# Fused attention and mixture of experts on one core: the stretch from the last features to the second expert written out as a given order, the first expert's weights loaded during attention, and two transposes issued by ScalarE

## The chip, the cores and the metric

The kernel runs on one core of a Trainium2 chip. The metric is the device time of one execution in microseconds; a profiled execution also shows a span (first to last instruction) and the clock that was granted to TensorE. The engines are TensorE (PE; its weight loads are PEld), VectorE (DVE), ScalarE (ACT), GpSimd (POOL) and SyncE (SP), which only starts transfers. ScalarE and GpSimd can start transfers too; each engine works through its own instructions in order, so a transfer that waits holds up what stands behind it.

## The reference

Eight batches, eight heads, sequence 576, head width 64. Attention has a decay from the running sum of `log f`; its output is the input of a mixture of eight experts, of which each row takes one.

```
scores = q @ k.T / sqrt(D) + cum[:, None] - cum[None, :]     # cum = cumsum(log(clip(f)))
scores = where(causal, -1e9, scores)                          # later keys are masked
attn   = exp(scores - rowmax); attn /= attn.sum() + 1e-9
x      = (attn @ v) as [4608 rows, 512]
e      = argmax(x @ w_gate)                                   # one expert per row
out[row] = gate(row) * eom(row, e) * (relu(x[row] @ w1[e]) @ w2[e])
```

## The kernel before

**Numbers in two halves.** Values that must be exact are kept as a high half (16 bits) and a low half (the rest), so a product with a weight takes three matmuls. A weight tile is loaded as float32 (256 KB), ScalarE casts the high half and another engine subtracts for the low half (`split_w1`, `split_w2`).

**Attention.** A unit is two heads, 32 units in all. A unit takes six steps of a hand-written list (`attention()`); the table `OFF` says at which step a piece of work starts, and `order` in which sequence the pieces of one step are emitted. All engines keep that order. For each unit the row maxima come first (`maxsteps`): products of K and Q in bf16 plus a correction by the tiles `Ek` and `Eq`, which carry the decay, plus two small products of `pick` and `negm` that push masked places of a diagonal 128x128 block to a large negative number: one over the second half of the rows and 128 columns, one over 64. The negated maxima go through a transpose and three small transfers (`max_put`) into the last row of each head's half of `Eq`. The scores (`score`) are made transposed in the same manner, with `pick` and `negt`. Then exp on ScalarE, the low half of p on GpSimd or VectorE (`expo`), the products with V (`head_av`) and the division. `Ek` and `Eq` exist five times; `blank` fills them in the prologue.

**Features and routing.** When four heads of a batch are done, `feats` casts the rows to a high and a low half, `feats_turn` transposes them by transfers of 128-row tiles into `xT`, and `feats_out` writes them to the DRAM buffer `xbuf`. Per batch, `route` multiplies `xT` with the gates (`lg`), picks the expert, ranks the rows within the expert (`rk`) and scatters (row number, weight) into the table `tbl` by one GpSimd transfer for each 128 rows. Batches 0 to 5 are routed during attention, 6 and 7 after it.

**Experts.** Each expert has room for 640 rows, five tiles. `gather_ids` reads the rows' numbers from `tbl`, `gather_rows` fetches the rows from `xbuf` into `xg`, `gather_turn` transposes them, `up` makes the eight products with W1 and their ReLU halves (`up_products` on TensorE; `up_split` on ScalarE and VectorE), `down` the products with W2, the scaling and the scatter to the output. For expert 0 the first three tiles are taken from batches 0 to 5 alone (`early_gather`), so that work is there before the last batches are routed; tiles 3 and 4 (`ET` to `CT`) follow when all are routed.

**The seam.** Between attention and the loop over experts stands a block whose order is given on all engines except GpSimd. It emits, in this sequence: the loads of the first four W2 tiles of expert 0; the last features (unit `NQ - 1`), their five transposes and their write; `route(B - 1)`, advanced by `OFF["steps"]` pieces between the eight up products of the three early tiles (one piece, the `lg` products, behind product 3; then 10 and 12); the W2 splits; the ids of the last two tiles; the loads of four W1 tiles of expert 1; `down` for the three early tiles; rows and transposes of tiles 3 and 4. What follows, from the products for tiles 3 and 4 on, is ordered by the framework's planner, as is `route(B - 2)`. The W1 tiles of expert 0 are fetched and split during the end of attention, from steps 169 and 177 on (attention ends at step 192).

The framework places semaphores: from data, from buffers that are used again, and between queues.

## Time and profile before

| | us |
|---|---|
| median of three runs | 843.28 (840.65 to 843.58) |
| the profiled execution | 842.0 |
| its span | 840.3 |
| TensorE busy in the span | 763.7 |
| GpSimd, ScalarE, VectorE busy | 479.8, 342.7, 332.2 |
| attention, first to last product with V | about 14 to 374 |
| seam | about 340 to 460 |

A line of the timeline reads: start, duration, engine, line of the kernel, operation, written tile <- read tiles, partitions and elements, count; in brackets the engine's idle time ahead of it and what ended it. Starts are microseconds from the span's start. Matmuls overlap, so two starts tell more than one duration. In a group's line the two numbers behind the bar are the busy time and the mean ns of one, then the idle time ahead. In the stage table come, behind the stage and its length, busy time and count of PE, PEld, DVE, ACT and POOL, then the granted clock, the transfers' share of the 16 engines, and GB/s.

### The profile page before, as it was taken

To read this page: it belongs to the slowest core of one execution; us is meant where nothing else is said; L and a number is where in the kernel's file an instruction comes from. 1 tells how busy PE (TensorE), PEld (TensorE's weight loads), DVE (VectorE), ACT (ScalarE), POOL (GpSimd) and SP (SyncE) were. 2 spreads that over 40 slices of the span, in tenths; PEclk is the share of its full clock that TensorE was granted. 3 is DMA by queue.
4 is the path that set the end of the run, shared out by engine and by line. 5 is a ranking of instruction groups with operands and counts; after the bars stand their busy time and mean duration, and the time that the engine had idled before them with its cause. 6 is when DMAs were issued, how large, how long until landed. Compare 5 with 4: busy or idle time off the path is not lost. (4 is left out here: it accounts for less than half of the span.)

```text
span 840.3 us, 21236 instructions
## 1 busy us (share of the span) xinstructions
PE 763.7 (91%) x8814; PEld 496.9 (59%) x8814; DVE 332.2 (40%) x760; ACT 342.7 (41%) x761; POOL 479.8 (57%) x508
## 2 busy tenths in 40 slices
PE   2799999999999999766928999999999999999996
PEld 1477776777777777543515665655656566565653
DVE  5455675757575766672501221202212031120310
ACT  4145564556555645451213432424334153331420
POOL 9278678798979897741365423725437264361301
PEclk9999999999999999997968999999999999999999
DMA  4233648585868685779679544655655556444201
GB/s 146 88 114 91 159 130 158 123 166 123 166 127 161 124 167 113 93 150 161 104 151 245 173 95 141 181 127 171 159 138 166 125 169 160 123 141 101 73 14 43
DMA packets 132920, 112.61 MB, mean 134 GB/s; under 512 B 96024, under 2 KB 105426, under 8 KB 132820
## 3 DMA queue, kind: packets, MB, share of 16 engines
q1 hardware_dynamic: 121092, 75.19, 41.4%
q0 software_dynamic: 7552, 18.92, 7.8%
q10 hardware_dynamic: 4176, 17.11, 7.7%
q8 instruction: 70, 1.15, 0.6%
q14 instruction: 30, 0.25, 0.1%
HBM read 72.79 MB, written 20.48 MB: 111 GB/s over the span
## 5 line engine op out<-in xcount | busy, mean ns | idle before, releaser
L373 POOL TENSOR_TENSOR plo<-p 128x512 f16<-128x512 f32 x186 | 193.2, 1053 | 56.6 <-ACT p L371 54.1
L902 PE MATMUL hp<-xT,w1h 128*128 128x384 f16 (+1 forms) x1024 | 199.5, 305 | 24.4 <-DMA xT<-xg 23.7
L289 DVE TENSOR_REDUCE nR<-mx 128x2 f32<-128x1024 f32 (+4 forms) x160 | 126.7, 809 | 103.6 <-PE mx L263 98.9
L371 ACT ACTIVATE p<-sc 128x512 f32<-128x512 f32 x192 | 112.5, 594 | 79.7 <-PE sc L263 75.9
L902 PEld LDWEIGHTS <-w1h 128*128 128x128 f16 x1024 | 101.5, 100 | 72.9 <-DMA xT<-xg 17.1
L912 DVE SCALAR_TENSOR_TENSOR hl<-hp,hh 128x256 f16<-128x256 f32 (+1 forms) x128 | 60.5, 491 | 185.1 <-ACT hh L911 184.8
L902 PE MATMUL hp<-xT,w1l 128*128 128x384 f16 (+1 forms) x512 | 130.7, 305 | 0.0
L263 PE MATMUL sc<-qk 64*128 64x512 f32 (+4 forms) x640 | 129.1, 472 | 1.1 <-issue 1.1
L930 PE MATMUL y<-w2h,hh 128*128 128x512 f16 x320 | 120.8, 381 | 4.1 <-ACT hh L911 4.1
L931 PE MATMUL y<-w2l,hh 128*128 128x512 bf16 x320 | 121.0, 381 | 0.0
L935 POOL DMA_INDIRECT out_dram<-ys,ids x40 | 41.6, 1039 | 138.9 <-ACT ys L934 105.7
L932 PE MATMUL y<-w2h,hl 128*128 128x512 f16 x320 | 118.8, 379 | 0.0
L263 PEld LDWEIGHTS <-pick 64*128 64x128 bf16 (+1 forms) x1152 | 62.0, 98 | 47.3 <-issue 25.9
L658 POOL TENSOR_TENSOR w1l<-w1r,w1h 128x512 bf16<-128x512 f32 x56 | 63.8, 1158 | 45.1 <-ACT w1h L657 43.9
L657 ACT CAST w1h<-w1r 128x512 f16<-128x512 f32 x64 | 39.5, 617 | 119.7 <-issue 64.2
L864 DVE TENSOR_TENSOR w2l<-w2r,w2h 128x512 bf16<-128x512 f32 x36 | 27.7, 772 | 148.5 <-ACT w2h L863 148.5
L934 ACT ACTIVATE ys<-y,ids 128x512 f32<-128x512 f32 x40 | 27.3, 686 | 123.9 <-PE y L932 91.7
L263 PE MATMUL mx<-qk 64*128 64x256 bf16 (+5 forms) x384 | 62.8, 309 | 14.7 <-DVE nR L289 8.9
L447 PE MATMUL av<-Vs,plo 128*128 128x65 f16 x640 | 68.9, 192 | 6.4 <-POOL plo L373 6.4
L445 PE MATMUL av<-Vs,p 128*128 128x65 f16 x640 | 69.7, 194 | 0.9 <-ACT xr L492 0.7
L446 PE MATMUL av<-Vs,p 128*128 128x64 bf16 x640 | 69.2, 195 | 0.0
L911 ACT ACTIVATE hh<-hp 128x256 f16<-128x256 f32 (+1 forms) x128 | 50.3, 432 | 40.9 <-PE hp L902 40.0
(148 smaller groups left out, 1395.6 us busy)
## 6 DMA issues: line engine op xcount, KB each, us to landing
qk<-in_qk_dram ACTq DMA_DIRECT2D x29, 576.0 KB
w1r<-in_w_dram SPq DMA_DIRECT2D x64, 256.0 KB
w2r<-in_w_dram SPq DMA_DIRECT2D x64, 256.0 KB
v<-in_vm_dram SPq DMA_DIRECT2D x16, 576.0 KB
xbuf<-x SPq DMA_DIRECT2D x16, 512.0 KB
qk<-in_qk_dram SPq DMA_DIRECT2D x3, 576.0 KB
xT<-x SPq DMA_TRANSPOSE x72
Eq<-mts SPq DMA_DIRECT2D x64, 0.1 KB
```

What stands on the lines that cost most here:

```text
L263: nc.tensor.matmul(dst(i), w(i), x(i), start=start, stop=stop)
L289: nc.vector.tensor_reduce(o, x, axis=AX.X, op=ALU.max, negate=True)
L371: nc.scalar.activation(out=f32, in_=src, func=AF.Exp, scale=0.125)
L373: eng.tensor_tensor(lo, f32, upper(f32), op=ALU.subtract)
L445: nc.tensor.matmul(dst, ph, vv[:, 0:W], start=kc == 0, stop=False)
L446: nc.tensor.matmul(dst[:, 0:D], ph, vv[:, W:].bitcast(BF16), start=False, stop=False)
L447: nc.tensor.matmul(dst, pl, vv[:, 0:W], start=False, stop=kc == qc)
L658: (eng or nc.vector).tensor_tensor(l, raw, h, op=ALU.subtract)
L902: nc.tensor.matmul(m[:, 0:(t1 - t0) * P], w[:, k], xT[:, t0:t1, k // 2, j, k % 2], start=k == 0 and i == 0, stop=k == ND - 1 and i == 2)
L930: nc.tensor.matmul(y, hh[:, fc, sl], wh, start=fc == 0, stop=False)
L931: nc.tensor.matmul(y, hh[:, fc, sl], wl, start=False, stop=False)
L932: nc.tensor.matmul(y, hl[:, fc, sl], wh, start=False, stop=fc == NF - 1)
```

## The change

It has five parts.

1. **Masks.** Four spare rows of each half of `Ek` and `Eq` now carry a mask for one quadrant of each diagonal block (-6e4 times 6e4). The `pick` products for 128 columns shrink to 64, in the row maxima and in the scores. For it `blank(0)` has four more selects on GpSimd, and the other copies of `Eq` are made on ScalarE from `plainq`.
2. **Weights of expert 0.** W1 and W2 tiles are loaded and split in attention, two of each around steps 48, 72, 96 and 120, each fetched ten steps ahead.
3. **Early rows.** The ids are read one step after batch 5 is routed (four before), the rows five steps after that (four before).
4. **The seam in a given order on all five engines**, from the last features to the weights of expert 1: the first two transposes of the last features stand ahead of the second half's casts; W1 tiles 0 to 3 of expert 1 are loaded before the routing, 4 to 7 later; the `lg` products stand behind product 5; ids of expert 1 come along with those of tiles 3 and 4; the low halves of W1 are made on VectorE; `down` for the early tiles is cut in two; the rows of expert 1 are fetched between the pieces. A GpSimd fill of one element stands between the last scatters.
5. **Two transposes of the last features** (tiles 1 and 3) are issued by ScalarE.

```diff
-    "feats0": 19, ... "rank": 6, "w1r": 169, "w1": 177, "w1step": 2,
-    "hold": 188, "gather": 180, "ids": 4, "landed": 4, ...
+    "feats0": 19, ... "rank": 6, "w1r": 10, "w1": 48, "w1step": 2, "w2": 4,
+    "hold": 188, "gather": 180, "ids": 5, "landed": 1, ...
-    "steps": [0, 0, 0, 1, 10, 12, 0, 0], "w2from": 1, ...
+    "steps": [0, 0, 0, 0, 0, 1, 8, 1], ...
...
     def blank(i, eng=nc.gpsimd):
-        eng.memset(Eqs[i], 1.0)
         if i == 0:
+            nc.vector.memset(Eqs[0], 1.0)
             nc.vector.memset(Eks[0], 0.0)
+            for h in range(HU):
+                sl = slice(h * D + 32, h * D + 32 + NC)
+                nc.vector.memset(Eqs[0][sl], 0.0)
+                for x, half, v in ((Eqs[0], 0, -6e4), (Eks[0], 1, 6e4)):
+                    x = x[sl, 0:SM].rearrange("p (c h k) -> p c h k", h=2, k=D)[:, :, half]
+                    nc.gpsimd.affine_select(out=x, in_=x, pattern=[[-1, NC], [0, D]], compare_op=ALU.not_equal,
+                                            fill=v, base=0, channel_multiplier=1)
...
         else:
             nc.gpsimd.tensor_copy(Eks[i], plain)
+            nc.scalar.copy(out=Eqs[i], in_=plainq)
...
         nc.gpsimd.tensor_copy(plain, Eks[0])
+        nc.scalar.copy(out=plainq, in_=Eqs[0])
...
-                    (lambda i: m[:, i, o + n - P:o + n], lambda i: pick[rows(i), 0], lambda i: negm[rows(i), 0],
+                    (lambda i: m[:, i, o + n - P:o + n - D], lambda i: pick[rows(i), 0], lambda i: negm[rows(i), 0, 0:D],
...
-            out += [(lambda i: dst(i)[:, 0:P], lambda i: pick[rows(i), 1], lambda i: negt[rows(i), 1], False, True)]
+            out += [(lambda i: dst(i)[:, D:P], lambda i: pick[rows(i), 1], lambda i: negt[rows(i), 1, D:], False, True)]
...
+            eng = nc.scalar if u == NQ - 1 and t % 2 else nc.sync
+            eng.dma_start_transpose(...)
...
+            if b == B - 1 and t:
+                nc.gpsimd.memset(apart, 0.0)
             ins = nc.gpsimd.indirect_dma_start(out=tbl, ...)
...
+    def early_split2(fc):
+        raw = W2r.pop(fc)
+        ...
+        nc.scalar.copy(out=h, in_=raw)
+        nc.vector.tensor_tensor(l, raw, h, op=ALU.subtract)
...
-    with tc.manual_schedule(engines=ENGINES - {mybir.EngineType.Pool}):
-        W2r = [fetch_w2(w2[0], fc) for fc in range(4)]
+    with tc.manual_schedule(engines=ENGINES):
         for part in range(2):
             feats(NQ - 1, part)
-        for t in range(NTB):
-            feats_turn(NQ - 1, t)
+            for t in (range(2), range(2, NTB))[part]:
+                feats_turn(NQ - 1, t)
         feats_out(NQ - 1)
+        W1r = [fetch_w1(m2, w1[1], fc, 4) for fc in range(4)]
         chain = route(B - 1)
         ...
         gather_ids(ar, tbl[EARLY:CAP], CT - ET, ET, x)
-        W1r = [fetch_w1(m2, w1[1], fc, 4) for fc in range(4)]
-        down(W2, x, h, 0, ET)
+        x1 = gather_ids(m2, tbl[NT:NT + CAP], CT)
+        W1n = [load_w1(w1[1], fc, W1r, nc.vector) for fc in range(4)]
+        down(W2, x, h, 0, 2)
         for t in range(ET, CT):
             gather_rows(x, t)
             gather_turn(x, t)
+        down(W2, x, h, 2, ET)
+        for t in range(2):
+            gather_rows(x1, t)
+        W1r += [fetch_w1(m2, w1[1], fc, 4) for fc in range(4, NF)]
+        up(W1, x, [(ET, CT)], h)
+        for t in range(2, CT):
+            gather_rows(x1, t)
+        for t in range(CT):
+            gather_turn(x1, t)
+        W1n += [load_w1(w1[1], fc, W1r, nc.vector) for fc in range(4, NF)]
+        down(W2, x, h, ET, CT)
+        W1, x = W1n, x1
+        W2 = weights(load_w2, w2[1])
```

More of the change, by code (lines that the diff above doesn't have):

```diff
@@ L55 @@
     "mturn": -7, "rows": -6, "put": -5, "rscore": 2, "rexp": 3, "av": 5, "fetch_v": (-19, -25, -21), "v": ((-2, -9, -16), (1, -7, -15)), "apart": 2, "scatter": 13,
-    "feats0": 19, "feats1": 20, "fturn": 21, "fturnstep": 2, "fout": 31, "route": 45, "rank": 6, "w1r": 169, "w1": 177, "w1step": 2,
-    "hold": 188, "gather": 180, "ids": 4, "landed": 4, "gturn": 2, "route_last": 200, "nsum": 8, "nrec": 9, "nx": 9, "nrest": 10,
+    "feats0": 19, "feats1": 20, "fturn": 21, "fturnstep": 2, "fout": 31, "route": 45, "rank": 6, "w1r": 10, "w1": 48, "w1step": 2, "w2": 4,
+    "hold": 188, "gather": 180, "ids": 5, "landed": 1, "gturn": 2, "route_last": 200, "nsum": 8, "nrec": 9, "nx": 9, "nrest": 10,
     "mv": ["xr", "v0", "v1"], "begin": -18, "wg": -4, "spread/1": -11,
-    "steps": [0, 0, 0, 1, 10, 12, 0, 0], "w2from": 1, "dve": [181, 183, 185, 187, 189, 191],
-    "w1pool": [0, 1, 2, 3, 4, 5, 6, 7],
+    "steps": [0, 0, 0, 0, 0, 1, 8, 1], "dve": [181, 183, 185, 187, 189, 191],
     "order": "reduce put feats1 v0 scores nrec max pair rows spread feats0 fetch "
@@ L113, in _attn_moe @@
     Eqs = [ab.tile([P, S], F16, name=f"Eq{i}") for i in range(NB)]
-    plain = ab.tile([P, S], F16, name="plain")
+    plain, plainq = [ab.tile([P, S], F16, name=n) for n in ("plain", "plainq")]
     Vs = [ab.tile([P, VC, 2 * D + 1], F16, name=f"Vs{i}") for i in range(3)]
@@ L171, in _attn_moe @@
     late = cp.tile([P, 1], F32, name="late")
+    apart = cp.tile([1, 1], F32, name="apart")
     identh = cp.tile([P, P], F16, name="identh")
@@ L523, in feats_turn @@
             xT, x16 = xTs[u]
-            nc.sync.dma_start_transpose(xT[:, t].rearrange("p j k n -> p (j k) n"),
-                                        x16[:, t].rearrange("p j n -> p (j n)"))
+            eng = nc.scalar if u == NQ - 1 and t % 2 else nc.sync
+            eng.dma_start_transpose(xT[:, t].rearrange("p j k n -> p (j k) n"),
+                                    x16[:, t].rearrange("p j n -> p (j n)"))
     def feats_out(u):
@@ L668, in early_split, with early_fetch2 @@
         W1.append(split_w1(ar, W1r.pop(fc), NF))
+    W2, W2r = [], {}
+    def early_fetch2(fc):
+        W2r[fc] = a.tile([P, DM], F32, name="w2r", bufs=2)
+        nc.sync.dma_start(W2r[fc], w2[0][fc])
+    def early_split2(fc):
+        raw = W2r.pop(fc)
+        h = ar.tile([P, DM], F16, name="w2h", bufs=NF)
+        l = ar.tile([P, DM], BF16, name="w2l", bufs=NF)
+        nc.scalar.copy(out=h, in_=raw)
+        nc.vector.tensor_tensor(l, raw, h, op=ALU.subtract)
+        W2.append((h, l))
     def gather_ids(pool, rows, n, t0=0, x=None):
@@ L716, in attention @@
         for fc in range(NF):
-            for f, o in ((early_fetch, "w1r"), (early_split, "w1")):
-                extra.setdefault(OFF[o] + OFF["w1step"] * fc, []).append((f, fc))
+            at = OFF["w1"] + 24 * (fc // 2) + OFF["w1step"] * (fc % 2)
+            extra.setdefault(at - OFF["w1r"], []).append((early_fetch, fc))
+            extra.setdefault(at, []).append((early_split, fc))
+            at += OFF["w2"]
+            extra.setdefault(at - OFF["w1r"], []).append((early_fetch2, fc))
+            extra.setdefault(at, []).append((early_split2, fc))
         for s in range(OFF["begin"], last + OFF["nrest"] + 1):
@@ L940, in weights, with load_w1 @@
         return [load(we, fc) for fc in range(NF)]
-    def load_w1(we, fc, raws=None):
-        return split_w1(m2, raws[fc] if raws and fc < len(raws) else fetch_w1(m2, we, fc, 4), 8, nc.gpsimd if fc in OFF["w1pool"] else None)
+    def load_w1(we, fc, raws=None, eng=nc.gpsimd):
+        return split_w1(m2, raws[fc] if raws else fetch_w1(m2, we, fc, 4), 8, eng)
     x = st["early"]
-    with tc.manual_schedule(engines=ENGINES - {mybir.EngineType.Pool}):
-        W2r = [fetch_w2(w2[0], fc) for fc in range(4)]
+    with tc.manual_schedule(engines=ENGINES):
         for part in range(2):
             feats(NQ - 1, part)
-        for t in range(NTB):
-            feats_turn(NQ - 1, t)
+            for t in (range(2), range(2, NTB))[part]:
+                feats_turn(NQ - 1, t)
         feats_out(NQ - 1)
+        W1r = [fetch_w1(m2, w1[1], fc, 4) for fc in range(4)]
         chain = route(B - 1)
@@ L956, in _attn_moe @@
         h = hidden()
-        W2 = []
         for fc in range(NF):
@@ L985, in _attn_moe @@
     halves = [(0, CT // 2), (CT // 2, CT)]
-    for e in range(E):
-        if e:
+    for e in range(1, E):
+        if e > 1:
             W2 = weights(load_w2, w2[e])
-            h = up(W1, x, halves)
-        else:
-            up(W1, x, [(ET, CT)], h)
+        h = up(W1, x, halves)
+        if e == 1:
             nsl = overflow_slots()
@@ L994, in _attn_moe @@
         if e + 1 < E:
-            W1 = [load_w1(w1[e + 1], fc, None if e else W1r) for fc in range(NF)]
+            W1 = [load_w1(w1[e + 1], fc) for fc in range(NF)]
             x = gather(m2, tbl[(e + 1) * NT:(e + 1) * NT + CAP], CT)
-        down(W2, xe, h, 0 if e else ET, CT)
+        down(W2, xe, h, 0, CT)
     with tc.For_i(0, nsl, 1) as i:
```

8 lines of the change are left out of this document (removed).

## The prediction

> **What bounds the kernel now.** I read the page's totals first, then the busy times by stage, then TensorE's waits in time order where a stage was not full. The page:
>
> ```profile
> span 840.3 us, 21236 instructions
> PE 763.7 (91%) x8814; PEld 496.9 (59%) x8814; DVE 332.2 (40%) x760; ACT 342.7 (41%) x761; POOL 479.8 (57%) x508
> ```
>
> The profiled execution took 842.0 us, 1.7 above its span and 1.3 below the median 843.28 of the three runs shown. TensorE leaves 76.6 us of the span. The stage table (busy us of each engine, then granted clock and DMA share) tells where:
>
> ```profile
> 252.00:300.00 48.00, 48.00 (x921) 36.22 (x919) 33.07 (x83) 28.97 (x69) 41.80 (x45) 1.00 0.74 155
> 340.00:360.00 20.00, 13.77 (x215) 9.54 (x212) 11.46 (x22) 9.75 (x22) 14.47 (x14) 0.91 0.92 92
> 380.00:400.00 20.00, 13.48 (x96) 7.81 (x97) 5.66 (x15) 3.81 (x9) 0.97 (x2) 0.76 0.98 165
> 420.00:440.00 20.00, 3.38 (x17) 1.41 (x16) 0.00 (x0) 3.06 (x5) 11.65 (x12) 0.63 0.72 141
> 440.00:460.00 20.00, 15.92 (x87) 9.98 (x86) 3.23 (x7) 6.60 (x13) 12.81 (x12) 0.77 1.11 237
> ```
>
> Inside attention (252 to 300) TensorE is full, GpSimd at 87%, VectorE 69%, ScalarE 60%. From 340 to 460, the seam, TensorE has holes and runs at a lower clock after each. TensorE's timeline there, with what ended each hole:
>
> ```profile
> 360.06 0.39 PE L263 MATMUL sc<-Eq,Ek 64*128 64x512 f16 x2 [1.12 <-DMA Eq<-mts]
> 381.36 0.80 PE L902 MATMUL hp<-xT,w1h 128*128 128x384 f16 x2 [7.11 <-DMA xT<-xg]
> 394.21 0.19 PE L556 MATMUL lg<-wgs,xT 128*128 128x32 f16 x1 [3.37 <-DMA xT<-x]
> 397.51 0.21 PE L556 MATMUL lg<-wgs,xT 128*128 128x32 f16 x1 [0.26 <-DMA xT<-x]
> 439.77 0.61 PE L902 MATMUL hp<-xT,w1h 128*128 128x256 f16 x2 [16.62 <-DMA xT<-xg]
> 449.14 0.61 PE L930 MATMUL y<-w2h,hh 128*128 128x512 f16 x1 [4.08 <-ACT hh L911]
> ```
>
> The holes stand for the early rows' transposes (7.1), the last features' transposes before the router (3.4, and smaller ones up to 397.5), the last two row tiles of expert 0 (16.6) and ReLUs queued behind weight casts (4.1).
>
> **The change part by part.** Times are on the clock of this profile.
>
> *Prologue.* Five fills of Eq leave GpSimd and VectorE; four small selects (4 partitions, 256 wide) are added on GpSimd, two 4-partition fills on VectorE, five copies of Eq on ScalarE.
>
> ```profile
> 2.11 0.28 POOL L181 TENSOR_SCALAR_AFFINE_SELECT pick<-pick 64x128 bf16<-64x128 bf16 x1
> 4.06 0.68 ACT L150 ACTIVATE d<-d 64x576 f32<-64x576 f32 x1 [1.96 <-DVE d L149]
> 6.83 1.93 POOL L127 TENSOR_SCALAR_AFFINE_SELECT Ek<-Ek 64x576 f16<-64x576 f16 x2
> 8.82 0.77 POOL L148 COPY plain<-Ek 128x576 f16<-128x576 f16 x1
> 9.62 3.75 SPq L162 DMA_DIRECT2D Ek<-d  x6
> 13.90 1.19 PE L263 MATMUL mx<-Ek,Eq 63*128 63x512 f16 x2 [7.50 <-DMA Ek<-d]
> ```
>
> The new copy plainq<-Eqs[0] stands in ScalarE's order ahead of the Ln at 4.06, and waits for three of the new selects, which GpSimd reaches at 6.83, or about a microsecond sooner if the scan no longer runs beside it. A select is between 0.28 (128 wide) and 0.97 (576 wide); I take 0.4. So Eqs[0] is ready near 7 to 8, the copy (0.66, the nearest rows are 0.6 to 0.8) ends near 7.5 to 8.7 and the Ln moves by 3.4 to 4.7. Behind it hang the scan, the three row copies and the six Ek<-d transfers, so TensorE's 13.90 moves as far. The shorter bound is GpSimd's own path, four selects ahead of plain: 1.7. I take **+3.4** (1.7 to 4.7).
>
> *Masks.* One matmul pair of each diagonal block shrinks from 128 to 64 columns, four blocks per unit in the row maxima and four in the scores:
>
> ```profile
> 330.12 0.20 PE L263 MATMUL mx<-qk 64*64 64x64 bf16 x2
> 330.15 0.20 PE L263 MATMUL mx<-Ek,Eq 63*64 63x64 f16 x2
> 335.40 0.22 PE L263 MATMUL mx<-qk 64*128 64x128 bf16 x2
> 335.45 0.22 PE L263 MATMUL mx<-Ek,Eq 63*128 63x128 f16 x2
> ```
>
> Read the starts, not the durations, which overlap: a pair of 64 columns holds TensorE 0.03 us, one of 128 columns 0.05 to 0.055. That is 0.025 x 8 x 32 units = 6.4 at most; the first units and the last two are not TensorE-bound. **-5** (-6.4 to 0: GpSimd at 87% could become the limit).
>
> *Weights of expert 0 into attention.* The eight W1 loads and splits move from steps 169 to 191 to four groups around steps 48, 72, 96 and 120; the eight W2 ones come with them from the seam.
>
> ```profile
> L657 ACT CAST w1h<-w1r 128x512 f16<-128x512 f32 x64 | 39.5, 617 | 119.7 <-issue 64.2
> L864 DVE TENSOR_TENSOR w2l<-w2r,w2h 128x512 bf16<-128x512 f32 x36 | 27.7, 772 | 148.5 <-ACT w2h L863 148.5
> L263 PE MATMUL sc<-Eq,Ek 64*128 64x512 f16 x56 | 11.2, 376 | 1.8 <-DMA Eq<-mts 1.8
> ```
>
> That is 16 x 0.617 = 9.9 on ScalarE, 16 x 0.772 = 12.4 on VectorE, sixteen SP issues and 4 MB, in a stage with 31% and 40% of these engines free and the DMA share at 0.74. If the cover fails, each group delays the row maximum's way to Eq; all such waits from 40 to 330 us are 1.8 now. I take **+2.5** (0 to 8). In return the end of attention loses the eight casts, splits and fetches between 339 and 369: the 1.12 wait at 360.06 goes, and two of these casts and splits (0.6 to 0.8 each) no longer stand in the short steps at its end, so all that follows comes about 2.5 earlier. I carry that in the next times instead of summing it.
>
> *Early rows.* With landed 1 and ids 5, the expert's ids are fetched three steps and the rows two steps sooner, so the first row transpose no longer stands behind the transposes of features 14, and the other two stand behind one of these instead of two.
>
> ```profile
> 369.50 1.19 SPq L524 DMA_TRANSPOSE xT<-x  x1
> 373.54 3.63 SPq L684 DMA_TRANSPOSE xT<-xg  x2
> 377.26 3.85 SPq L524 DMA_TRANSPOSE xT<-x  x3
> 383.32 3.20 SPq L857 DMA_DIRECT2D w2r<-in_w_dram  x4
> 387.33 8.90 SPq L524 DMA_TRANSPOSE xT<-x  x5
> 385.00 0.49 ACT L911 ACTIVATE hh<-hp 128x384 f16<-128x384 f32 x1 [7.59 <-PE hp L902]
> 386.89 0.49 ACT L911 ACTIVATE hh<-hp 128x384 f16<-128x384 f32 x1 [1.40 <-PE hp L902]
> 391.67 0.62 ACT L863 CAST w2h<-w2r 128x512 f16<-128x512 f32 x1 [4.29 <-DMA w2r<-in_w_dram]
> ```
>
> The three are issued by about 371 instead of 377.2 and land 4.2 later, as now (377.2 to 381.36): the first up product starts at 375.
>
> *The last five transposes.* Without the four w2r issues the first starts near 378.5 instead of 387.33. SP's queue still holds the feature writes ahead of it, and transfers queued at 383.3 landed at 391.6, so it lands at about 387. Tiles 1 and 3 are now ScalarE's. No row shows a transpose started there, and the kernel leaves all waits to its framework. The bounds are no wait at all, and a wait for the landing at each of four changes of queue. On SP's queue one is 1.24 of issue and at least 1.3 until landing (the last of the five is issued by 396.2 and used at 397.51), 2.5 together; the longest is 1.3 + 4.2 = 5.5. I take the wait, at 2.5. The Trainium skill, DMA: Bandwidth & Descriptors, "Silent corruption: two transposing streams in flight at once", says that a stream of transposes from the one queue has to wait until that of the other has landed in full; no run here shows it yet. By that rule the seam is the sum below, without it the first rival.
>
> With the wait, tile 1 is issued at 387, tile 2 at 389.5, tile 3 at 392; tile 4 lands at 397. ScalarE's order is cast, tile 1, casts, tile 3, ReLUs: it stands still until 393.3. Two up products fit the two PSUM buffers (375 to 380); the third waits for the first ReLU, so until 393.8. Then four products at 1.9 (ReLU rows 385.00 and 386.89) and 1.5 for the cold clock reach 403, the router's 1.0 gives 404, two more products 408.
>
> *From the rank to the last rows of expert 0.*
>
> ```profile
> 401.41 0.18 PE L598 MATMUL rk<-oh,before 128*128 128x40 bf16 x1
> 404.58 0.98 POOL L637 DMA_INDIRECT tbl<-rec,pi  x1 [0.50 <-DVE so L625]
> 422.15 0.38 SPq L674 DMA_DIRECT2D ids<-tbl  x1
> 422.58 1.89 SPq L651 DMA_DIRECT2D w1r<-in_w_dram  x4
> 426.35 1.05 POOL L678 DMA_INDIRECT xg<-xbuf,ids  x1 [14.44 <-issue]
> 433.92 2.65 SPq L684 DMA_TRANSPOSE xT<-xg  x2
> ```
>
> Now the chain is 3.2 (rank to scatter) + 17.6 (five scatters landed, ids issued) + 4.2 + 7.6 + 5.8 (to 439.77) = 38.4. The W1 loads of expert 1 come before it in the new order, which I put at 5 off the last three terms (1.7, 2.2 and 1.1, towards the 2 to 3 that an unhurried transfer takes from issue to use); the scatters I leave. So 408 + 33.4 = 441.5, **+1.7** against 439.77. Behind it the order helps: W1 casts no longer stand between the products and their ReLUs, **-4.1**, and the slow clock is paid once (3.4 us at half speed, 1.7) and not from 439.8 to 444.9 and from 449.1 to 452.6 (4.3): **-2.6**. The tiny GpSimd fills between scatters (0.1 each) I cost at nothing, as they stand where the chain waits for landings anyway.
>
> Sum: 3.4 - 5 + 2.5 + 1.7 - 4.1 - 2.6 = -4.1. 842.0 - 4.1 = 837.9 in a profiled execution, and 843.3 - 4.1 = **839** as a median. Its own range is 833 to 845.
>
> **The rivals.**
> 1. *The queues do not wait for each other.* Then ScalarE is free from 380, the products run through from 375, the router's at 389 when tiles 2 and 4 have landed, the rank at 394, the last rows at 427: 14 earlier than above. 825. For it: the new steps put the router after six products, which suits data at 388. Against it: nothing in the trace shows two such queues side by side.
> 2. *Slower: the hand-over is dear.* If each change of queue costs 5.5, as the early rows' landing does, tile 3 is issued 6 later and with tile 1 also late by 3, ScalarE is free 9 later; nothing lies beside that wait, so the rank and all behind it are 9 later. 848. It decides from 5.2 a hand-over on (8.2 us over three).
> 3. *The weights' transfers reach the row maxima.* For it: DMA at 0.74 and bursts of 1 MB just where the scatters lie. If three groups each hold two units by 1.5, +9 instead of +2.5: 845. Against: the 1.8 of such waits in all.
> 4. *The masks bring nothing* because GpSimd or the row-maximum reduction sets the pace: 844.
>
> **How the numbers follow.** Forecast 0.50, half of it on either side of 839; rival 1 0.15; a milder form of it, with ScalarE's wait short because tile 0 lands early, 0.08 at 831; rival 2 0.13; rivals 3 and 4 0.14. About 0.5%, 4.2 us, is what a measurement of this kernel can tell from no change, so faster means below 839.1: 0.25 + 0.15 + 0.08 = 0.48. Slower, above 847.5: 0.13 + 0.06 = 0.19. Same: 0.33. The range takes in rivals 1 and 2: 824 to 848.
>
> **What would show it.** Start: the first mx<-Ek,Eq near 17. Masks: a full unit 0.2 shorter. Seam: ScalarE without work from about 375 to 393, with its transposes at its two ends; the third up product held by a ReLU; the last rows' hole ending near 441; no ReLU wait behind it. The prediction is wrong if ScalarE's transposes start while SP's are in flight, if the scatters' 17.6 shrinks because the W2 loads no longer share the queue, or if units in attention exceed their 10 us where the weights come in.

## The result, and the profile after

The changed kernel has a median of 851.27 us (846.53 to 854.24, six runs) where the kernel before had 843.00 beside it (839.85 to 845.32, six runs): a ratio of 1.012, 95% interval 1.009 to 1.015. The forecast was 839. The profiled execution is the quickest of the six, 846.53 us with a span of 844.8. First the page's totals:

```profile
span 844.8 us, 21246 instructions
PE 766.0 (91%) x8814; PEld 499.2 (59%) x8814; DVE 349.1 (41%) x770; ACT 344.0 (41%) x767; POOL 473.9 (56%) x504
```

TensorE does the same work; VectorE has 16.9 us more in ten more instructions. The stage table of after:

```profile
252.00:300.00 48.00, 45.14 (x835) 34.04 (x833) 34.04 (x80) 26.42 (x63) 38.39 (x40) 0.96 0.71 133
380.00:400.00 20.00, 11.29 (x172) 7.49 (x169) 7.01 (x30) 4.26 (x13) 6.14 (x7) 0.80 0.47 67
400.00:420.00 20.00, 15.22 (x120) 9.00 (x120) 5.43 (x15) 3.78 (x10) 0.00 (x0) 0.77 0.58 155
420.00:440.00 20.00, 15.43 (x73) 6.89 (x71) 8.24 (x24) 4.69 (x10) 9.67 (x14) 0.99 0.13 28
440.00:460.00 20.00, 10.68 (x80) 8.76 (x81) 2.12 (x5) 2.30 (x6) 8.77 (x9) 0.66 1.00 233
```

In attention (252 to 300) TensorE is no longer full: 45.1 of 48 us at a clock of 0.96, where before had 48.0 at 1.00. The stretch from 420 to 440, nearly empty before (3.4 us), is now filled; the stretches on both sides of it have the holes. TensorE's timeline at these holes:

```profile
17.41 0.58 PE L273 MATMUL mx<-Ek,Eq 63*128 63x512 f16 x1 [11.13 <-DMA Ek<-d]
389.78 0.80 PE L936 MATMUL hp<-xT,w1h 128*128 128x384 f16 x2 [4.62 <-DMA xT<-xg]
404.78 0.80 PE L936 MATMUL hp<-xT,w1h 128*128 128x384 f16 x2 [8.19 <-DVE hl L946]
449.32 0.61 PE L936 MATMUL hp<-xT,w1h 128*128 128x256 f16 x2 [13.89 <-DMA xT<-xg]
```

The third up product (404.78) waits 8.2 us for a ReLU's halves. What held that ReLU stands on ScalarE's timeline, then SP's:

```profile
395.99 1.29 ACTq L536 DMA_TRANSPOSE xT<-x  x1
397.32 0.62 ACT L527 CAST x<-x 128x512 f16<-128x512 f32 x1 [9.72 <-issue]
402.32 1.23 ACTq L536 DMA_TRANSPOSE xT<-x  x1
403.65 0.87 ACT L945 ACTIVATE hh<-hp 128x384 f16<-128x384 f32 x2 [5.40 <-issue]
387.00 14.02 SPq L536 DMA_TRANSPOSE xT<-x  x4
405.96 3.83 SPq L536 DMA_TRANSPOSE xT<-x  x3
```

ScalarE computes nothing for 9.7 and then 5.4 us around its two transposes. That was forecast. The loss in attention, 13 us by the start of the last unit, was not. TensorE's waits from 42 to 330 us, two lines of after, then the largest of before:

```profile
PE av L455 <- ACT xr L502: 6.3, 9, 2.9
PE av L455 <- DVE x L145: 3.3, 2, 1.7
```

```profile
PE sc L263 <- DMA Eq<-mts: 1.8, 1, 1.8
```

Products with V now wait for the normalized rows (`x`, `xr`), where before had no such wait. One of these places on GpSimd, VectorE, ScalarE and TensorE:

```profile
129.30 2.49 POOL L383 TENSOR_TENSOR plo<-p 128x512 f16<-128x512 f32 x2
129.55 1.35 DVE L696 TENSOR_TENSOR w2l<-w2r,w2h 128x512 bf16<-128x512 f32 x1
130.82 0.41 DVE L495 TENSOR_TENSOR x<-av,sm 128x256 f32<-128x256 f32 x1
131.26 0.62 ACT L527 CAST x<-x 128x512 f16<-128x512 f32 x1 [1.61 <-DVE x L495]
132.40 0.31 ACT L502 ACTIVATE xr<-av,sm 64x64 f32<-64x64 f32 x1
132.76 0.19 PE L455 MATMUL av<-Vs,p 128*128 128x65 f16 x1 [0.67 <-ACT xr L502]
```

The low half of a W2 tile (1.35 us) stands ahead of a head's normalization (130.82); ScalarE's cast waits 1.61 us for that, its `xr` comes behind the cast, and TensorE's next product behind `xr`. The subtract itself is long because GpSimd works beside it: it starts while GpSimd makes a low half of p (`plo`) and ends 0.55 us behind that one's end at 130.35. All eight W2 subtracts here start so and end 0.55 behind GpSimd's instruction, 0.72 to 1.35 us long, where one without such a neighbour takes 0.69.

### The profile page after: what moved, and what is told of

The parts are those of the page before. It is cut to its first block, busy times and chain, and to the rows that moved or that the text cites. A ratio compares the mean times of both kernels' runs of the same rounds, so it can differ in the third digit from the quotient of the medians.

```text
span 844.8 us, 21246 instructions
## 1 busy us (share of the span) xinstructions
PE 766.0 (91%) x8814; PEld 499.2 (59%) x8814; DVE 349.1 (41%) x770; ACT 344.0 (41%) x767; POOL 473.9 (56%) x504
## 5 line engine op out<-in xcount | busy, mean ns | idle before, releaser
L383 POOL TENSOR_TENSOR plo<-p 128x512 f16<-128x512 f32 x186 | 197.6, 1077 | 70.5 <-ACT p L381 66.2
L936 PEld LDWEIGHTS <-w1h 128*128 128x128 f16 x1024 | 101.5, 99 | 76.2 <-issue 18.7
L273 PE MATMUL sc<-qk 64*128 64x512 f32 (+4 forms) x640 | 136.4, 486 | 0.0
L273 PEld LDWEIGHTS <-pick 64*128 64x128 bf16 (+1 forms) x1152 | 64.2, 99 | 46.8 <-issue 24.7
L273 PE MATMUL mx<-qk 64*128 64x256 bf16 (+5 forms) x384 | 64.7, 312 | 14.6 <-DVE nR L299 8.9
L673 POOL TENSOR_TENSOR w1l<-w1r,w1h 128x512 bf16<-128x512 f32 x48 | 55.1, 1165 | 38.5 <-ACT w1h L672 38.4
```

The source lines that it names most:

```text
L273: nc.tensor.matmul(dst(i), w(i), x(i), start=start, stop=stop)
L383: eng.tensor_tensor(lo, f32, upper(f32), op=ALU.subtract)
L936: nc.tensor.matmul(m[:, 0:(t1 - t0) * P], w[:, k], xT[:, t0:t1, k // 2, j, k % 2], start=k == 0 and i == 0, stop=k == ND - 1 and i == 2)
```

## The experiments

The table gives what each kernel measured. The ratio is to the kernel before on the same chip; the other columns are read from the one profiled execution of each, in us: the last unit's first score product with `Eq` against before's, then, counted from the last product with V, the last logits, the first up product of the last rows, and the last matmul. One execution can lie some us off its kernel's median (the twelfth unit alone takes 15.4 us in after and 10.8 in e4, whose attention is the same but for the prologue), so where the two differ the ratio decides. From e5 on, every kernel but e8 and e12, which start from before, has all of the last five transposes on SP's queue.

| kernel | ratio, 95% interval | last unit | logits | last rows | end |
|---|---|---|---|---|---|
| before | 1 | 0 | 23.7 | 65.8 | 459.6 |
| after | 1.0120 (1.009 to 1.015) | +13.0 | 30.8 | 64.5 | 453.1 |
| e1_weights_late | 1.0072 (1.004 to 1.010) | -2.8 | 30.5 | 70.0 | 457.1 |
| e2_shift | 1.0063 (1.003 to 1.010) | +11.5 | 31.1 | 65.3 | 452.2 |
| e3_one_queue | 0.9946 (0.991 to 0.998) | +14.8 | 18.8 | 53.0 | 441.8 |
| e4_prologue | 1.0089 (1.006 to 1.012) | +7.6 | 30.7 | 66.0 | 455.5 |
| e5_one_queue_late | 1.0043 (1.001 to 1.007) | +2.4 | 25.9 | 68.7 | 460.3 |
| e6_no_transfers | 0.9948 (0.992 to 0.998) | +12.6 | 18.0 | 50.6 | 438.1 |
| e7_w1_late_w2_mid | 0.9936 (0.990 to 0.997) | +6.2 | 20.1 | 54.8 | 442.1 |
| e8_before_two_queues | 1.0102 (1.006 to 1.014) | -0.4 | 31.6 | 70.7 | 461.9 |
| e9_spaced | 0.9953 (0.993 to 0.998) | +12.5 | 20.3 | 55.3 | 443.2 |
| e11_no_subtract | 0.9843 (0.980 to 0.988) | +0.9 | 18.6 | 51.8 | 440.0 |
| e12_masks | 0.9993 (0.996 to 1.002) | +1.1 | 22.7 | 60.0 | 452.6 |
| e13_gpsimd | 1.0017 (0.999 to 1.004) | +15.2 | 18.2 | 51.2 | 438.8 |
| e14_spaced_gpsimd | 1.0190 (1.015 to 1.023) | +16.3 | 18.7 | 55.0 | 442.9 |
| e15_late_gpsimd | 1.0013 (0.999 to 1.004) | -1.8 | 26.4 | 65.8 | 453.5 |
| e16_raws | 0.9911 (0.988 to 0.994) | +3.2 | 20.0 | 55.6 | 443.9 |
| e17_raws_gpsimd | 0.9908 (0.987 to 0.994) | +1.0 | 17.8 | 52.2 | 439.5 |

My theory at first was that the weights' transfers cost the attention, by meeting the scatters of the table and waiting in the queues.

**The weights back where they were.** W1 at steps 169 to 191, W2 between the products of the seam:

```diff
-            at = OFF["w1"] + 24 * (fc // 2) + OFF["w1step"] * (fc % 2)
...
+            extra.setdefault(169 + 2 * fc, []).append((early_fetch, fc))
+            extra.setdefault(177 + 2 * fc, []).append((early_split, fc))
...
+            if fc:
+                early_split2(fc - 1)
```

> The kernel after, with the weights of the second part put back: W1 of expert 0 fetched at steps 169 to 183 and split at 177 to 191, W2 fetched and split between the first up products of the seam; everything else as after. Theory 1 (the 32 transfers and splits between steps 38 and 140 cost the attention some 15 us, because they meet the scatters of the routing table): the units from 9 to 27 return to 9.76 us, the last unit starts some 13 us earlier, and the time falls to about 838 (836 to 842), since part of the seam's gain of 8.5 us goes with the splits that return to it. Rival 2 (the loss lies in the changed seam or in the transposes on ScalarE's queue): the units get shorter by a few tenths at most and the time stays within 849 to 853. Rival 3 (the attention is longer whatever the weights do, from the masks or from ScalarE's copies): the long units 10, 12, 14, 22 remain.

The units return to 9.76 us and the last one starts 2.8 earlier than in before: the loss in attention is due to the early loads and splits. The time falls by less than expected, 4 us by the ratio and 7.3 in the traces. There the last value product comes 11.3 earlier, and the seam gives back 4.0 of it (the last rows come 5.5 later).

**The groups ten steps later.**

```diff
-"w1r": 10, "w1": 48,
+"w1r": 10, "w1": 58,
```

> The kernel after, with all groups of weights ten steps (16 us) later: fetched at steps 48 to 54, split at 58 to 64, and so on by 24, where after has 38 to 44 and 48 to 54. Theory 1 (it is the meeting of the transfers with the scatters at steps 58 to 68 of every 24 that costs): the transfers now stand in steps without scatters, the units 9 to 27 together lose 8 to 13 of their 15 us, and the time is about 841 (838 to 845). Rival 2 (the work of the splits on ScalarE and VectorE costs it, wherever they stand): the long units move by one or two, their sum stays, and the time is within 2 of 851.

The last unit is still 11.5 late; the long units only move. The ratio, 1.0063, is lower than after's 1.0120, with intervals that just meet. Most of the loss in attention does not hang on the transfers meeting the scatters.

**All five transposes on SP's queue.**

```diff
-            eng = nc.scalar if u == NQ - 1 and t % 2 else nc.sync
+            eng = nc.sync
```

> The kernel after, with all of the last five transposes on SP's queue. Theory 1 (a transposing transfer waits for the one before it on the other queue, and ScalarE stands with it): the stretch in which ScalarE issues the two transposes (387.6 to 396 and 398.2 to 402.3 us) is gone, the third up product no longer waits 8.2 us for its ReLU, the router's logits come 3 to 5 us earlier, and the time falls to about 847 (844 to 850). Rival 2 (the two queues do not wait for one another, and what ScalarE waits for is the hole in the features): the logits come no earlier, the time is 851 to 853. Rival 3 (the third product's hold is given back by the hole before the last rows, which goes by the logits alone): the hold is gone and the time within 1 of 851.

Theory 1, by more than expected: the logits come 12.0 earlier, and the ratio falls from 1.012 to 0.9946, 0.0174 or 14.6 us. The five go out one behind another on SP, ScalarE's first ReLU is at 395.04, and the wait of the products for the ReLU's halves is 0.2 in place of 8.2:

```profile
396.18 7.65 SPq L536 DMA_TRANSPOSE xT<-x  x5
395.04 0.49 ACT L945 ACTIVATE hh<-hp 128x384 f16<-128x384 f32 x1 [4.77 <-issue]
```

```profile
PE hp L936 <- DVE hl L946: 0.2, 1, 0.2
```

**The prologue's copy behind the activations.**

```diff
         nc.scalar.activation(late[0:B * H], lf[:, 0:1], AF.Exp)
+        nc.scalar.copy(out=plainq, in_=Eqs[0])
```

> The kernel after, with the copy of the plain query mask on ScalarE placed behind the two activations of the prologue (logarithm and exponential) in place of ahead of them. Theory 1 (that copy holds the logarithm, and the rest of the first unit's delay is VectorE's longer row of memsets): the first unit starts 1.0 to 2.0 us earlier than in after, 1.1 to 2.1 later than in before, and the time falls by as much, to about 849.8. Rival 2 (the delay comes from GpSimd's selects and copies of the masks alone): the first unit starts within 0.3 of after's, no change in the time.

The first unit starts 1.2 earlier than in after, as theory 1 has it. The ratio's interval overlaps that of after, so the time alone does not show it.

**Both undone.** The edits of the first and third run together:

> The kernel after with both edits of the first two runs that undo a part: all of the last five transposes on SP's queue, and the weights of expert 0 loaded as in before (W1 at steps 169 to 191, W2 between the products of the seam). The queue alone moved the ratio to before from 1.012 to 0.995, the weights alone to 1.007. Theory 1 (two costs in different places, which add up): 0.990, some 829.5 us where before has 838. Rival 2 (with the router early, the splits of W2 between the products of the seam become what the last rows wait for): the last rows' turns no earlier than in the kernel with the queue alone, measured from the last value product (53 us), and 0.995 or more.

Rival 2. The two costs do not add up: the logits are 25.9 behind the last value product, not 18.8. ScalarE's timeline tells why; a cast of W2 waits for its transfer and the ReLU stands behind it:

```profile
392.14 0.62 ACT L694 CAST w2h<-w2r 128x512 f16<-128x512 f32 x1 [7.53 <-DMA w2r<-in_w_dram]
392.67 0.48 ACT L940 ACTIVATE hh<-hp 128x384 f16<-128x384 f32 x1
```

**The splits without the transfers.**

```diff
-        W1r[fc] = fetch_w1(a, w1[0], fc, 3)
+        W1r[fc] = W1r[0] if fc else fetch_w1(a, w1[0], fc, 3)
```

and the same for W2.

> The kernel after with all of the last five transposes on SP's queue, and with only the first block of W1 and of W2 fetched: all eight splits of each read that one tile, at the same steps. 14 of the 16 transfers of 256 KB are left out (expert 0 is computed with wrong weights); the work of the splits on ScalarE and VectorE stays whole. To be compared with the kernel that has the queue alone (last unit 14.8 us later than in before, ratio 0.995). Theory 1 (the transfers cost the attention, through the queues and DMA engines that they share with the small transfers): the units from 9 to 27 fall back to lengths as of before or shorter, the last unit starts no later than in before (between -4 and +1), and the ratio is about 0.978 to 0.985. Rival 2 (the splits hold ScalarE and VectorE): the long units remain and the last unit is still 10 or more later, the ratio 0.993 or more. In between: each has its share, as the start of the last unit shows.

My first theory falls: 14 transfers fewer, and the ratio is the same as with them (0.9948 against 0.9946), the last unit 12.6 late.

**W1 late, W2 in the middle.**

```diff
+            extra.setdefault(139 + 2 * fc, []).append((early_fetch2, fc))
+            extra.setdefault(143 + 2 * fc, []).append((early_split2, fc))
```

> The kernel after with all of the last five transposes on SP's queue, the prologue's copy of the query mask behind the two activations, W1 of expert 0 where before has it (steps 169 to 191), and W2 at two steps for each block from step 139 (units 23 to 26), split four steps behind. It keeps what the seam gained (no load of W2 in it) and takes the loads out of the units 6 to 22. Theory 1: the units to 22 as in the kernel with late weights, a loss of 2 to 5 us in the units 23 to 27, the seam from the last value product to the end 441 to 443 us as with the queue alone, so about 0.983 (0.979 to 0.988). Rival 2 (the loads cost the same wherever they stand among the units): a loss of 8 us from unit 23 on, half of what 16 loads cost, and 0.990 or more.

Rival 2: the lateness of the units grows by about 8 us in the units where the eight splits stand (0.5 at unit 24, 8.2 at unit 27), so about one us for each split, at another place as well.

**The transposes alone, in the kernel before.** The same choice of queue as in after, put into the kernel before:

> The kernel before, with the second and fourth of the last five transposes issued by ScalarE, and nothing else changed. Theory 1 (a transposing transfer waits for the one before it on the other queue, whatever the order of the work around it): the last logits come some 10 to 12 us later behind the last value product (23.7 us in before), ScalarE stands some 8 to 12 us in all at its two issues, and the ratio is 1.010 to 1.016. Rival 2 (the cost belongs to the order of the work in after, where both feature parts are mixed with transposes): the logits within 3 us of before's, and a ratio within 0.004 of 1. Rival 3 (the logits are late, but the hole before the last rows swallows it): logits 10 later and a ratio below 1.006.

Theory 1, though the logits are 7.9 later where 10 to 12 were expected; the ratio is 1.0102. ScalarE's timeline, then SP's:

```profile
386.53 6.22 ACTq L525 DMA_TRANSPOSE xT<-x  x2
379.19 16.00 SPq L525 DMA_TRANSPOSE xT<-x  x3
```

SP issues tile 0 at 379.19 and ScalarE tile 1 at 386.53; from there to ScalarE's second issue (6.22 less 1.21 of its own) there are two changes of queue, 2.5 us each. The first took 7.3: ScalarE waited in turn for three of SP's transposes, two of the early rows and tile 0, and the last of them landed at 386.43.

**The splits spaced evenly, or behind the normalization.** One split each six steps, at steps without a normalization; and the group's steps kept, with the splits emitted later within a step:

```diff
-"fetch_v fturn extra tick mturn tick v1 nx rexp
+"fetch_v fturn tick mturn tick v1 nx extra rexp
```

> The kernel after with all of the last five transposes on SP's queue, the prologue's copy of the query mask behind the two activations, and the 16 loads of expert 0 spread evenly, one each six steps: W1 split at steps 47, 59, ... 131, W2 at 53, 65, ... 137, each fetched ten steps ahead (after has groups of four, at steps 48, 50, 52, 54 and so on by 24). Step 47 and those by six behind it are ones in which VectorE has no normalization of a head to issue and no pair of row maxima. Theory 1, formed on the runs so far (the split's VectorE subtract of 0.95 to 1.35 us, issued at step 54 ahead of a head's normalization, holds that, then ScalarE's copy of it and the value products behind that; the transfers are innocent): the gaps of 0.8 to 1.9 us at value products go, the units 8 to 22 are within 0.3 of those of the kernel with late weights, the last unit starts 2 to 5 earlier than in before, and the ratio is about 0.978 (0.974 to 0.985). Rival 2 (16 splits cost about 1 us each wherever they stand, because VectorE and ScalarE have no such room): the last unit still 8 or more later, the ratio 0.990 or more.

> The kernel after with all of the last five transposes on SP's queue, and with one change in the order of the work within a step: the loads and splits are issued behind the head's normalization (nx) instead of ahead of the route's steps and of it. Their steps stay. Theory 1 (a split ahead of the normalization holds the value products): the units 9, 13, 17 and 21 lose 1 us or more each, the last unit starts 6 to 12 earlier than in the kernel with the queue alone (14.8 later than in before), and the ratio is 0.981 to 0.988. Rival 2 (the split delays the row maxima or the router's steps instead, or VectorE is full in these units): the long units stay within 0.5, ratio 0.993 or more.

Both miss: 0.9953, and 0.9934 (0.990 to 0.997) for the order, which the interval cannot tell from 0.9946. The wait moves: with even spacing TensorE waits for the row maxima's reductions, from 42 to 340 us, and the last unit is still 12.5 late. So it is not the one place. And half of the evenly spaced subtracts fall behind a run of GpSimd's instructions: the one that starts at 147.40 stands beside three of GpSimd's low halves in a row and lasts 3.60 us. The 16 together take 29.2 us in this kernel and 16.3 in after, where 16 times 0.69 would be 11.0. The groups ten steps later (e2) took 29.9, so spacing and shifting made the subtracts themselves longer, and neither run tests places without that. The profiled execution of e10_order is the longest of its twelve, so the table leaves it out.

```profile
PE mx L273 <- DVE nR L299: 8.0, 8, 1.9
```

**No subtracts.**

```diff
-        W1.append(split_w1(ar, W1r.pop(fc), NF))
+        h = ar.tile([P, ND, P], F16, name="w1h", bufs=NF)
+        nc.scalar.copy(out=h, in_=W1r.pop(fc))
+        W1.append((h, zl.rearrange("p (k n) -> p k n", k=ND)))
```

> The kernel after with all of the last five transposes on SP's queue, and without VectorE's half of the early splits: one tile of zeros stands for the lower part of all blocks of expert 0's weights (its rounding is left out of the result). All 16 transfers and ScalarE's 16 casts stay where they are. Theory 1 (VectorE's subtract is what costs): the last unit starts between 4 earlier and 2 later than in before, ratio 0.978 to 0.985. Rival 2 (ScalarE's casts cost as much): the last unit 6 to 9 later, ratio about 0.988. Rival 3 (ScalarE's casts alone): 13 or more later, 0.994.

Theory 1: with all transfers and all casts in place the last unit is 0.9 late in place of 14.8, and the ratio falls by 0.0103, 8.6 us. VectorE's subtracts are the cost. The zeros are first multiplied behind attention, so they cannot be what brings the last unit forward. The two sizes differ because the profiled execution with the subtracts lies 5.5 above its median and the one without 2.2 below.

**The masks alone.** The first part of the change, in the kernel before:

> The kernel before with the first part of the change alone: the causal masks that the first contraction takes over, the narrower products of the masks, and the copies of the two plain masks in the prologue. By the terms of the prediction: the first unit 3.1 later (3.4 forecast), undisturbed units 9.76 in place of 9.92, 4.5 to 5 over all units, so the last unit 1.5 to 2 earlier than in before, and a ratio of 0.998. Rival (a unit of another length meets the routing's transfers and steps at other times, and gains or loses more by that than by its products): the last unit off that by over 3 to either side.

No measurable change (0.9993). In the trace, unit 27 is 0.9 earlier, as the terms say, and the last is 1.1 later, since one unit at the end took longer; the rival may have a part in it. The interval, 2.5 us to either side, cannot tell the forecast's 0.998 from 1.

**The subtracts on GpSimd**, in the groups and evenly spaced:

```diff
-        W1.append(split_w1(ar, W1r.pop(fc), NF))
+        W1.append(split_w1(ar, W1r.pop(fc), NF, nc.gpsimd))
```

> The kernel after with all of the last five transposes on SP's queue, and with the 16 early subtracts of the splits on GpSimd in place of VectorE, at the same steps. To be compared with the kernel with the queue alone (0.995, last unit 14.8 later than in before) and that without the subtracts (0.984, 0.9 later). Theory 1 (it is VectorE's time that is short in the units): the last unit 0 to 5 later than in before and a ratio of 0.984 to 0.988. Rival 2 (any engine of the attention's chain: GpSimd's subtract of 1.1 us delays the lower halves of the probabilities, which the value products wait for): the last unit 10 or more later, waits of the value products for plo, ratio 0.993 or more.

> The kernel with the loads spread evenly (one each six steps), one queue and the prologue's copy behind the activations, with the 16 subtracts on GpSimd. The same kernel with VectorE had a ratio of 0.995 and the last unit 12.5 later than in before. Theory 1 (VectorE's time): last unit 0 to 4 earlier, ratio 0.979 to 0.985. Rival 2 (GpSimd's time is as short): 8 or more later, 0.992 or more.

Theory 1 misses twice: it gets worse (1.0017 and 1.0190; the six executions of the second lie between 839 and 855, so only its direction counts). The numbers are those of the rivals, but not by the way that the first of them names: waits for `plo` are 0.4 us in all, and the longest waits of TensorE from 42 to 330 us in the groups' kernel are still for VectorE:

```profile
PE mx L273 <- DVE nR L299: 8.0, 17, 0.6
PE av L457 <- POOL plo L383: 0.4, 2, 0.2
```

The reason is in the table of stages for the units 8 to 23 (length; busy us and count of PE, PEld, DVE, ACT, POOL), of before, after, the kernel without transfers, without subtracts, and with GpSimd's, in this order:

```profile
114.10:282.40 168.30, 164.81 (x3160) 123.37 (x3158) 110.41 (x277) 94.05 (x228) 142.91 (x151) 1.00 0.71 144
```

```profile
116.00:297.00 181.00, 170.36 (x3158) 127.28 (x3156) 126.89 (x292) 99.89 (x243) 147.01 (x150) 0.98 0.76 151
```

```profile
116.20:292.40 176.20, 169.87 (x3162) 126.39 (x3160) 127.38 (x293) 99.96 (x243) 147.36 (x151) 0.98 0.64 138
```

```profile
115.90:285.20 169.30, 164.41 (x3162) 123.39 (x3160) 110.86 (x277) 100.34 (x243) 143.54 (x151) 0.99 0.76 162
```

```profile
115.80:299.40 183.60, 169.54 (x3162) 125.00 (x3160) 126.21 (x277) 99.59 (x243) 162.54 (x167) 0.98 0.71 149
```

Read the DVE column. Without subtracts VectorE is busy 110.9 us with 277 instructions. With GpSimd's subtracts it has the same 277 instructions, and they take 126.2. Which ones, VectorE's timeline and then GpSimd's show:

```profile
116.77 0.86 DVE L596 TENSOR_TENSOR oh<-cand,sc 128x32 bf16<-128x32 f32 x1
117.67 0.96 DVE L599 TENSOR_TENSOR tmp<-L,oh 128x32 f32<-128x32 f32 x1
126.69 0.84 DVE L631 CAST pi<-sc 128x4 int32<-128x4 f32 x1
116.42 1.16 POOL L673 TENSOR_TENSOR w1l<-w1r,w1h 128x512 bf16<-128x512 f32 x1
117.54 1.04 POOL L383 TENSOR_TENSOR plo<-p 128x512 f16<-128x512 f32 x1
126.34 1.16 POOL L696 TENSOR_TENSOR w2l<-w2r,w2h 128x512 bf16<-128x512 f32 x1
```

Each of the three ends within 0.1 us of GpSimd's instruction that ran when it started: 117.63 and 117.58, 118.63 and 118.58, 127.53 and 127.50. In the kernel without subtracts, the second of them starts in a gap of GpSimd's, between an instruction that ends at 116.58 and one that starts at 117.13:

```profile
117.11 0.19 DVE L599 TENSOR_TENSOR tmp<-L,oh 128x32 f32<-128x32 f32 x1
```

So work given to GpSimd comes back as VectorE's time. The row-maximum reductions, which read PSUM, are not touched: over these units they take 64.6 us without subtracts and 64.5 with GpSimd's. The Trainium skill, "SBUF — State Buffer", section "SBUF: two separate sides", says that GpSimd and such VectorE instructions as run in a two-port mode or read two inputs from SBUF take turns at a pair of ports, and that the one which comes second stands until the other's instruction is done, and "Perfetto Trace Analysis", "Optimizing Scalar/DVE Operations", that moving work between these two might therefore not help; these rows agree.

**The splits in the seam, late transfers or early ones.** W2's subtracts in the seam on GpSimd, with W2 still fetched there; then W2 fetched in attention, one tile each four steps from 125 on, into eight tiles that stay, and split behind the eight up products:

```diff
+            extra.setdefault(125 + 4 * fc, []).append((early_fetch2, fc))
...
             up_split(hp, h, first, fc)
+            early_split2(fc)
```

> The kernel with the weights of expert 0 where before has them and all five transposes on SP's queue (1.004), with the prologue's copy behind the activations and the subtracts of W2 in the seam on GpSimd, which has no work there until the last batch's records. Theory 1 (in that kernel VectorE's eight subtracts and ScalarE's casts between the products delayed the router): the logits 19 to 21 behind the last value product in place of 25.9, the end 443 to 446 behind it in place of 460, the last unit 0 to 3 earlier than in before, ratio 0.982 to 0.987. Rival 2 (ScalarE's casts are what delays it, or the scatters then wait for GpSimd): the end 455 or more behind the last value product, ratio 0.997 or more.

> The kernel after with all of the last five transposes on SP's queue, the prologue's copy behind the two activations, W1 of expert 0 where before has it, and W2 of expert 0 fetched one tile each four steps from step 125 on into eight tiles that stay; the casts and subtracts of W2 are made in the seam, one behind each of the first eight up products, the subtracts on VectorE. Theory 1 (transfers cost nothing in the attention, subtracts do, and in the seam it was the late transfers that held ScalarE's casts): the last unit 1 to 4 earlier than in before, the end 441 to 447 behind the last value product, ratio 0.978 to 0.986. Rival 2 (the casts and subtracts themselves hold the ReLUs and the router in the seam): the last unit as early, but the logits 24 or more behind the last value product and the end 452 or more, ratio 0.993 or more.

> The same with the subtracts of W2 on GpSimd. Theory 1: as the kernel with VectorE's subtracts within 3 us. Rival 2 (VectorE's subtracts hold the router): logits 2 or more earlier than with VectorE's. Rival 3 (GpSimd's subtracts stretch VectorE's small steps of the router, as in the attention): logits 2 or more later than with VectorE's.

With late transfers rival 2 holds by the ratio, 1.0013, and the logits at 26.4; the end, 453.5, is just short of its 455. GpSimd's subtracts did not bring the router forward, and TensorE now waits 8.0 us for them ahead of the products with W2. With the tiles at hand the casts stand between the ReLUs and hold nothing: ScalarE waits for TensorE alone.

```profile
390.88 0.49 ACT L942 ACTIVATE hh<-hp 128x384 f16<-128x384 f32 x1 [1.40 <-PE hp L933]
391.27 0.61 ACT L695 CAST w2h<-w2r 128x512 f16<-128x512 f32 x1
392.83 0.49 ACT L942 ACTIVATE hh<-hp 128x384 f16<-128x384 f32 x1 [0.95 <-PE hp L933]
```

The logits stand at 20.0 and 17.8, and the ratios are 0.9911 and 0.9908, alike for both engines within their intervals: **these two beat both kernels**, before by 0.9% (0.6 to 1.3) and after by some 2%. They are the lowest of the kernels that keep both halves of all weights, but their intervals overlap those of e3, e7 and e10. The logits are 2.2 earlier with GpSimd's subtracts, which is rival 2's sign (VectorE's subtracts hold the router a little); the time does not show it. Expected was 0.978 to 0.986; the last unit starts 3.2 and 1.0 later than in before where 1 to 4 earlier were expected. What holds the units around 27 there is open. In the first of the two, TensorE's only wait from 280 to 345 us is 2.9 for the row maxima's transfer into `Eq`, in the queue where W2's loads now stand too; no run tests whether these made it.

## Why the prediction was wrong

*The step that failed is the term "Weights of expert 0 into attention", +2.5.* In the profiled execution it should have been some 14: the last unit starts 13.0 late, of which the prologue explains 3.5 and the masks take off 4.8. By the ratios, the subtracts alone are 8.6 us, give or take 4, and the transfers nothing that can be told from zero. The forecast's sum of -4.1 with 14.3 in place of 2.5 gives +7.7, and the medians differ by +8.3, but this nearness is partly luck: that execution was only 4.5 us longer than before's. There the last product with V came 10.9 late where the forecast had 1.6 early, and the rest of the kernel gained 6.5 where the forecast, counted from that product, had 2.5. Two things were wrong in the term. The cover: 31% of VectorE's time was free, and the term took this as room. But VectorE's reductions and normalizations lie in a chain with TensorE (the row maxima have one buffer, the value products wait for `xr`), so an instruction in between moves the chain: 16.5 us more of VectorE's busy time became 12.7 us of length over the units 8 to 23. How much of a subtract becomes length depends on what stands behind it: e2 and e9 had 29 to 30 us of subtracts and lost no more. And the price: the term had 12.4 us for the 16 and they took 16.3. Its 0.772 was a mean in which most rows lie in the experts' stage. In attention, beside GpSimd's subtracts, the same instruction takes more than in the seam, where GpSimd only starts transfers, as two groups of after show, from 42 to 330 us and from 440 us on:

```profile
L696 DVE TENSOR_TENSOR w2l<-w2r,w2h 128x512 bf16<-128x512 f32 x8 | 8.4, 1055 | 0.0
L673 DVE TENSOR_TENSOR w1l<-w1r,w1h 128x512 bf16<-128x512 f32 x4 | 2.5, 686 | 0.1
```

Rival 3 had the place, with units over 10 us, but the wrong cause (transfers); that its 9 us lie near the 8.6 by the ratios is luck.

*Prologue, +3.4:* right. TensorE's first `mx<-Ek,Eq` moved from 13.90 to 17.41.

*Masks, -5:* right by the trace: undisturbed units took 9.76 in place of 9.91, times 32 units 4.8. The time of the kernel with the masks alone is too close to before's to show it.

*Five transposes:* the mechanism was right. The third up product was held by a ReLU behind ScalarE's transposes. The rank was put at 408 with the last value product at 371.4, 36.6 behind it; it came 34.7 behind it. The price of one change of queue was right for two of the four, 2.5; one took 3.6 and the first 7.6 (SP's last issue ahead at 388.35), and ScalarE's tiles went between those of the features before, so the near total is in part luck. Rival 1, queues that do not wait, was put 14 lower; putting the five on one queue, which is another way to be rid of the wait, gained 14.6. The rule of the Trainium skill that the forecast took up ("DMA: Bandwidth & Descriptors", "Silent corruption: two transposing streams in flight at once") agrees with this trace: ScalarE's first transpose was issued at 395.99, 0.1 us after the last of SP's ahead of it had landed. What the forecast did not say is that this part by itself loses 1.0% in the kernel before.

*Rank to last rows, 33.4:* it took 29.8, to 449.32, by two errors that partly cancel. The "five scatters landed" that were left at 17.6 took 11.0, from the first scatter to the ids' fetch, as GpSimd's and SP's rows of after show; this was named as a point where the sum might fail, with the W2 loads as the reason, which no run singled out. From the ids' fetch to the products, put at 12.6 with W1's loads out of the way, it took 16.1, so most of that gain of 5 did not come.

```profile
422.17 1.48 POOL L652 DMA_INDIRECT tbl<-rec,pi  x1 [0.51 <-DVE runs L639]
433.19 3.16 SPq L703 DMA_DIRECT2D ids<-tbl  x3
```

*No casts ahead of the ReLUs, -4.1:* right, no such wait is left. *Slow clock paid once, -2.6:* right behind the last rows, where TensorE ran at half its pace once, from 449.3 to 453.1; the granted clock is 0.66 at 440 to 460. Ahead of them, around the hold of 8.2, the clock is low too, 0.80 and 0.77 from 380 to 420. From the last rows' first product to the end it took 5.2 less than before; these two terms said 6.7.

## What to carry to other kernels

An engine's free share in a stage is no cover for new work on it when its instructions lie in a chain with the engine that sets the pace: ask which instruction will stand ahead of which, and take the price of one from rows in the same stage. A subtract on VectorE also takes what GpSimd's instructions beside it make of it, here 0.69 to 3.60 us. The loads could come early for little, so long as the splits stood where VectorE and GpSimd had time; and keep transposing transfers on one queue, away from an engine whose ReLUs others wait for.

## What was not expected of the hardware

- Small VectorE instructions that started beside a GpSimd subtract lasted until that was done: 0.17 to 0.19 became 0.84 to 0.96 us, and 277 VectorE instructions over 16 units cost 15.4 us more when 16 subtracts were given to GpSimd.
- Fourteen more transfers of 256 KB in attention, at a DMA share of 0.76 (after) against 0.64, changed the time by nothing that can be measured (0.9946 against 0.9948, each within 0.003).
- A change of queue between two transposing transfers cost 2.5 to 3.6 us with one or two of the other queue under way, and 7.3 to 7.6 with three.
- A 128x512 subtract on VectorE took 0.69 us alone and up to 3.60 us beside three GpSimd subtracts in a row.
